# Sigmoid-gate products of two groups as 64-row pairs inside the up burst, with the attention stages two steps later

## The chip, the cores and the metric

The kernel runs on one core of a Trainium2 chip. The metric is the device time of one execution in microseconds (us), as the median of several runs. The engines are TensorE (PE in the profile; its weight loads are PEld), VectorE (DVE), ScalarE (ACT), GpSimd (POOL) and SyncE (SP, which issues the transfers here). Each engine takes its own instructions in the order in which the program gives them, and waits on semaphores for the others.

## The reference

The input x has the shape (4, 12608, 128). First comes an attention through 32 inducing vectors, then a channel mix in which every token also sees the one before it:

```python
def _attn_ref(x, inducing):
    def mab(q, kv):
        s = scale * (q @ kv.transpose(0, 2, 1)); s = s - s.max(-1, keepdims=True)
        a = np.exp(s); a /= a.sum(-1, keepdims=True) + 1e-09
        return a @ kv
    h = mab(I, x)              # 32 inducing vectors look at all tokens of a batch
    return mab(x, h)           # every token looks at the 32 results

def _moe_ref(x, mu_k, mu_r, w_k, w_v, w_r):
    x_prev = ...               # x moved by one token
    xk = mu_k * x + (1.0 - mu_k) * x_prev
    xr = mu_r * x + (1.0 - mu_r) * x_prev
    k = np.maximum(xk @ w_k, 0.0)          # d_ff = 1024
    v = k * k @ w_v
    r = 1.0 / (1.0 + np.exp(-(xr @ w_r)))  # the sigmoid gate
    return r * v
```

## The kernel before

**Groups, units, steps.** The tokens of a batch are cut into 25 groups of 512 tokens (the last one of a batch has 320). Since every token is a mix of only 32 results h, the products with w_k and w_r are folded into products of h with them: a token is represented by its 32 attention weights and by those of the token before it, 64 rows in all. These rows, as a rounded part (index 0) and the rest (index 1), lie in the tile R of the group, and twice: in partitions 0 to 63 and again in 64 to 127. The folded weights W (for k, as W[0] and W[1]) and Wg (for the gate) have 64 rows and lie twice likewise.

A group has 4 units of work, for 256 of the 1024 hidden columns each. The main loop has one step n for each unit, 400 in all (4 batches of 25 groups of 4). In the loop a step does, in this order in the program of each engine: `gate` of a finished group on DVE (L823); in even steps the *burst* of `up` products of this and the next unit on PE (L788); the `early` events of the step (registered with `soon`); `square` (L798 relu on DVE, L803 and L805 squares on ACT, or L800 on DVE in place of L803 in the steps of `high_vector`; then the difference kl on POOL, L808); in the second step of a group, `zgate`; `store` (L834); the `down` products of the unit of four steps ago on PE (L818); and the `events` of the step (registered with `at`).

`up` has 6 matmuls of 64 rows per unit: three terms (W[0] by R part 0, W[1] by part 0, W[0] by part 1), each once on rows 0 to 63 and once on rows 64 to 127, into the two banks of a `ps_a` tile. That makes 12 per burst of two units. `down` has 6 matmuls of 128 rows per unit, into the group's bank `ps_v`. `zgate` has 2 matmuls of 128 rows (L776) into the same `ps_v` bank, which the sigmoid (L778) empties into rT before the group's first `down` fills it again. The lower half of Wg holds the rest of the upper half there, so that 128 rows give two of the terms at once.

**PSUM.** It has 8 banks: two `ps_a` tiles of two banks, two `ps_v` banks in turn, `pb_a` and `pb_b`. A tile that is asked for under a name whose only bank is in use makes its first writer wait for the last reader of the tile before.

**The attention stages.** They run in the same loop, on a calendar. A batch b has segments of 12 steps (`SEG`); segment j begins at step s = 100b + 12j (4 + 12j for b = 0). I call n - s the place of step n in its segment. In segment j, `stage_a(b + 1, j)` works on block j (four groups) of the next batch, and `stage_b(b, j + 1)` makes the R tiles of block j + 1 of this one.

- Stage A with its offsets from s: four DVE transposes `btr` and their transfers to xt on SP (-1, 0, 1, 3); `scores` (9) on PE into `pb_a` (L367), its maximum on DVE; `expo` (15, early) on ACT, which reads `pb_a` (L403, L404); `etrans` (16) on DVE; `hmm` (17) on PE into a new `pb_a` (L436); `acc` (19) on DVE, which reads it. Offsets of 12 and more fall in the next segment. The last block has a tail (`t_tr` at 8 in `pb_a`, `t_scores`, `t_etrans` in `pb_b`).
- Stage B from s + 1: `scores` (0) on PE into `pb_b` (L617), then softmax on DVE in `pb_b` with its exponential (3, at the end of the step) on ACT (L634), `high` on ACT (7 after s), `low` on DVE (10 after s), then `spread`: transfers on SP that fill R of a new group, and two steps later `double`, which copies the upper 64 rows to the lower. R has 5 buffers, so `spread` of group f waits for the last reader of group f - 5.
- After the six segments of a batch `combine` makes h and the folded weights of the next one in `pb_b` and `pb_a`.

The 31 table loads at L778 in the profile are ACT's change from the set of functions with exp to the one with sigmoid.

Of the kernel before, what the change touches and what calls it, by code (L numbers as in the profile page):

```python
# [8 lines left out]
F32 = mybir.dt.float32  # L9
# [10 lines left out]
def kernel(  # L20
# [43 lines left out]
    banks = iter("ab" * 64)  # L64

    def pb_tile(bank=None):
# [142 lines left out]
    def stage_a_head(j):  # L209
# [34 lines left out]
        def scores():  # L244
            L.s1 = pv.tile([P, G], F32, name="ps_v")
# [75 lines left out]
    def stage_a(b, j, at, t):  # L321
# [139 lines left out]
        at(t + 10 + tail, common)  # L461
        at(t + 11 + tail, running)
        soon(t + 15, expo)
        at(t + 16, etrans)
        if tail:
            at(t + 16, t_etrans)
        at(t + 17, sums)
        at(t + 17, lambda: hmm(0))
        at(t + 17, lambda: hmm(1))
        at(t + 17, t_hmm)  # L470
        at(t + 19, acc)
        k = order_a.index((b, j))
# [8 lines left out]
    def combine(b, at=None, t=0):  # L481
# [45 lines left out]
        def hfin():  # L527
            ps = pb_tile("b")
            nc.tensor.matmul(out=ps[:, :M], lhsT=S.acc, rhs=L["sw"], start=True, stop=True)
            S.hT = sm.tile([P, M], F32, name="hT")  # L530
            nc.vector.tensor_copy(out=S.hT, in_=ps[:, :M])
            h4 = L["h4"] = sm.tile([P, Q, M], F32, name="h4", bufs=1)
            for n, mu in enumerate((muk, omuk, mur, omur)):
                nc.vector.tensor_scalar(out=h4[:, n, :], in0=ps[:, :M], scalar1=mu, scalar2=None, op0=ALU.mult)
            S.W = [wp.tile([P, F // 2], F32R, name=f"W{s}") for s in range(2)]
            S.Wg = wp.tile([P, C], F32R, name="Wg")

        def wpart(gate, tile):


            X = {}
            cw = C if gate else F // 2
            rows = slice(HP if gate else 0, P)

            def prod():
                X["ps"] = tile()[:, :cw]
                chunks = wk_sb.rearrange("p (c e d) -> p e c d", e=2, d=P)
                for n in range(Q):
                    o = X["ps"][M * n:M * (n + 1), :]
                    if not gate:  # L550
                        o = o.rearrange("m (c d) -> m c d", d=P)
                    nc.tensor.matmul(out=o, lhsT=L["h4"][:, 2 * gate + n % 2, :],
                                     rhs=wr_sb if gate else chunks[:, n // 2], start=True, stop=True)

            def high():
                nc.scalar.copy(out=(S.Wg if gate else S.W[0]), in_=X["ps"])

            def low():
                hi, lo = (S.Wg, S.Wg) if gate else S.W
                nc.vector.tensor_tensor(out=lo[rows], in0=X["ps"][rows], in1=hi.bitcast(F32)[rows],  # L560
                                        op=ALU.subtract)
            return prod, high, low

        if ahead:
            return maxes, weights, weights_sum, hfin, wpart
        at(t + 8, weights)
        at(t + 9, hfin)
        for gate in range(2):
            prod, high, low = wpart(gate, lambda: pb_tile("a"))
            at(t + 10 + 2 * gate, prod)  # L570
            at(t + 10 + 2 * gate, high)
            at(t + 11 + 2 * gate, low)

# [185 lines left out]
    NG = (NBLK - 1) * Q + 1  # L759
    UB = NG * NU  # L760

    class Group:
        def __init__(self, b, g):
# [4 lines left out]
            self.v = None  # L768

        def zgate(self):  # L770

            S, w = self.S, self.w
            R = S.R[self.g]
            ps = self.v = pv.tile([P, G], F32, name="ps_v")[:, :w]
            for s in range(2):
                nc.tensor.matmul(out=ps[:, :w], lhsT=S.Wg, rhs=R[:, s, :w], start=(s == 0), stop=(s == 1))  # L776
            self.rT = mp.tile([P, G], F32, name="rT")[:, :w]
            nc.scalar.activation(out=self.rT, in_=ps[:, :w], func=AF.Sigmoid)  # L778

        def up(self, u):  # L780
# [3 lines left out]
            ps = self.ps[u] = pa.tile([P, UC, G], F32, name="ps_a")  # L784
            for n, (a, k) in enumerate(((0, 0), (1, 0), (0, 1))):
                for r in range(2):
# [23 lines left out]
        def down(self, u):  # L810
            w = self.w
            if self.v is None:
                self.v = pv.tile([P, G], F32, name="ps_v")[:, :w]
            kh, kl = self.h.pop(u)
# [10 lines left out]
        def store(self):  # L825
# [10 lines left out]
            if g % span == span - 1 or g == NG - 1:  # L836
# [132 lines left out]
    def start():  # L969

        def bank():
            return pv.tile([P, G], F32, name="ps_v")

        wk = wpart(0, bank)
        wg = wpart(1, bank)
        (sc0, df0, ex0, nm0, turn0, hi0, lo0, idle), *rest = [stage_b_first(g) for g in range(Q)]
# [37 lines left out]
    end = len(units) - 1  # L1014
    late = []
    with tc.manual_schedule():
        head()
        start()
        for n in range(len(units) + LAG + 2):
            grp, u = units[n] if n < len(units) else (None, n % NU)  # L1020
            old, ou = units[n - LAG] if LAG <= n < len(units) + LAG else (None, 0)
            m = n - LAG - 1
            if 0 <= m < len(units) and units[m][1] == NU - 1:
                units[m][0].gate()
            if grp is None:
                run(late)
                late = []
            else:
                if n % 2 == 0:
                    for g, v in units[n:n + 2]:  # L1030
                        g.up(v)
                run(early.pop(n, []))
                whole = n in (end - 3, end - 1, end)
# [7 lines left out]
            if 1 <= m <= len(units) and units[m - 1][1] == NU - 1:  # L1041
                units[m - 1][0].store()
            if old is not None:
# [32 lines left out]
```

## Time and profile before

| | |
|---|---|
| median of 3 runs | 1096.88 us (1095.34 to 1097.85) |
| the profiled execution | 1095.42 us, span 1093.4 us |
| granted TensorE clock, mean | 0.999 |
| PE busy | 1068.4 us (98%), 6622 matmuls |
| DVE, ACT, POOL busy | 909.0, 961.2, 944.2 us (83, 88, 86%) |

The profile is of one execution; its own time is 1.46 us under the median. A busy PE is counted from matmuls that overlap in their records, so that the time from one start to the next is what a matmul costs when they follow each other.

### The profile page before, as it was taken

How to read it: one execution, taken by the hardware profiler on the slowest of the kernel's cores; microseconds unless marked ns; L12 is line 12 of the kernel's file. 1: busy time of each engine (PE TensorE's matmuls, PEld its weight loads, DVE VectorE, ACT ScalarE, POOL GpSimd, SP SyncE). 2: the span in 40 equal slices, each digit the busy share in tenths (PEclk: the TensorE clock that was granted, in tenths of full speed). 3: DMA queues.
4: the chain of work that ended last, by engine and by line, in shares of the span. 5: the costliest groups of instructions: out<-in, count | busy, mean ns of one | idle time of the engine just before them, and what ended most of it. 6: DMA issues, size and time to landing. Idle time of an engine off the chain costs nothing.

```text
span 1093.4 us, 19337 instructions
## 1 busy us (share of the span) xinstructions
PE 1068.4 (98%) x6622; PEld 735.1 (67%) x6622; DVE 909.0 (83%) x1296; ACT 961.2 (88%) x1101; POOL 944.2 (86%) x419
## 2 busy tenths in 40 slices
PE   7889999999999999999999999999999999999998
PEld 5456666666676666666676666666767666667776
DVE  4799899997788999997778899998786888887665
ACT  5498989898999889898999888999989989999996
POOL 2278988898889988989888989889889899999996
PEclk9999999999999999999999999999999999999999
DMA  9305676674157576665245746764415434453422
GB/s 280 118 8 116 157 158 163 142 157 100 27 113 168 122 163 134 145 156 126 41 75 121 171 109 150 176 149 102 86 28 108 83 59 93 85 101 70 89 40 35
DMA packets 267634, 123.61 MB, mean 113 GB/s; under 512 B 225648, under 2 KB 247056, under 8 KB 265232
## 3 DMA queue, kind: packets, MB, share of 16 engines
q1 hardware_dynamic: 267200, 122.35, 50.9%
q8 instruction: 53, 0.87, 0.4%
q14 instruction: 45, 0.37, 0.1%
q10 hardware_dynamic: 336, 0.02, 0.0%
HBM read 28.07 MB, written 25.82 MB: 49 GB/s over the span
## 4 chain that ended last, share of the span: by engine, by line
PE 84%; ACT 6%; DVE 3%; issue 2%; POOL 2%; SPq 1%; DMA 1%; ACTq 0%; DVEq 0%; POOLq 0%
PE ps_v L818 49%; PE ps_a L788 25%; PE ps_v L776 4%; ACT kh L803 2%; PE pb_b L617 2%; POOL kl L808 2%; PE pb_a L367 2%; PE pb_a L436 2%; ACT k_t L805 1%; DVE k_t L798 1%; DMA kl<-in_x_dram 1%; SPq L188 1%; ACT L778 1%; SPq L95 1%; ACT L634 0%
## 5 line engine op out<-in xcount | busy, mean ns | idle before, releaser
L808 POOL TENSOR_TENSOR kl<-k_t,kh 128x1024 fp32r<-128x1024 f32 (+1 forms) x397 | 932.6, 2386 | 105.8 <-ACT k_t L805 98.5
L798 DVE TENSOR_SCALAR k_t<-ps_a 128x1024 f32<-128x1024 f32 (+1 forms) x400 | 477.1, 1198 | 97.1 <-PE ps_a L788 74.7
L805 ACT ACTIVATE k_t<-k_t 128x1024 f32<-128x1024 f32 (+1 forms) x397 | 415.2, 1050 | 51.5 <-DVE kh L800 18.1
L803 ACT ACTIVATE kh<-k_t 128x1024 fp32r<-128x1024 f32 (+1 forms) x352 | 365.1, 1037 | 44.4 <-DVE k_t L798 41.7
L788 PE MATMUL ps_a<-R,W 64*128 64x512 f32 (+1 forms) x2400 | 331.1, 407 | 5.2 <-DVE k_t L798 4.5
L788 PEld LDWEIGHTS ps_a<-R,W 64*128 64x128 f32 x2400 | 208.7, 184 | 126.6 <-issue 49.5
L818 PE MATMUL ps_v<-kh,wvh 128*128 128x512 f32 (+1 forms) x800 | 270.3, 419 | 2.1 <-ACT rT L778 2.1
L818 PE MATMUL ps_v<-kh,wvl 128*128 128x512 f32 (+1 forms) x800 | 248.6, 392 | 0.0
L818 PE MATMUL ps_v<-kl,wvh 128*128 128x512 f32 (+1 forms) x800 | 248.5, 392 | 0.0
L818 PEld LDWEIGHTS ps_v<-kh,wvh 128*128 128x128 f32 x800 | 133.8, 188 | 93.0 <-issue 48.7
L818 PEld LDWEIGHTS ps_v<-kh,wvl 128*128 128x128 f32 x800 | 149.7, 188 | 34.9
L818 PEld LDWEIGHTS ps_v<-kl,wvh 128*128 128x128 f32 x800 | 149.5, 188 | 34.9
L823 DVE TENSOR_TENSOR oT<-ps_v,rT 128x512 f32<-128x512 f32 (+1 forms) x100 | 66.9, 669 | 20.4 <-PE ps_v L818 20.2
L834 DVE STREAM_TRANSPOSE ot<-oT 128x512 f32<-128x512 f32 x96 | 66.9, 697 | 0.0
L776 PE MATMUL ps_v<-R,Wg 128*128 128x512 f32 (+1 forms) x200 | 63.3, 398 | 0.0
L800 DVE SCALAR_TENSOR_TENSOR kh<-ps_a,k_t 128x1024 fp32r<-128x1024 f32 x48 | 58.8, 1225 | 1.7
L778 ACT ACTIVATE rT<-ps_v 128x512 f32<-128x512 f32 (+1 forms) x100 | 57.9, 579 | 0.3
L339 DVE STREAM_TRANSPOSE xs<-xb 128x512 f32<-128x512 f32 x72 | 49.9, 693 | 0.6 <-DMA xb<-in_x_dram 0.2
L776 PEld LDWEIGHTS ps_v<-R,Wg 128*128 128x128 f32 x200 | 36.5, 188 | 8.6 <-issue 0.8
L778 ACT ACT_TABLE_LOAD x31 | 39.8, 1283 | 0.6
L617 PE MATMUL pb_b<-xt,hT 128*32 128x512 f32 x184 | 24.4, 603 | 1.0 <-DVE R L749 1.0
L663 DVE TENSOR_TENSOR hl<-pb_b,hl 128x512 fp32r<-128x512 f32 x23 | 15.8, 688 | 7.0 <-ACT hl L660 6.7
(216 smaller groups left out, 527.0 us busy)
## 6 DMA issues: line engine op xcount, KB each, us to landing
out_dram<-ot SPq DMA_DIRECT2D x184, 128.0 KB, 2.7
R<-R SPq DMA_DIRECT2D x88, 256.0 KB, 3.0
xb<-in_x_dram SPq DMA_DIRECT2D x18, 1024.0 KB, 5.5
xt<-xs SPq DMA_DIRECT2D x288, 64.0 KB, 2.0
R<-hl SPq DMA_DIRECT2D x96, 128.0 KB, 2.3
R<-hl SPq DMA_DIRECT2D x96, 127.8 KB, 2.4
kh<-in_x_dram SPq DMA_DIRECT2D x4, 512.0 KB, 7.9
kl<-in_x_dram SPq DMA_DIRECT2D x4, 512.0 KB, 7.4
```

Source lines behind the costliest of these rows:

```text
L339: nc.vector.transpose(out=xs.rearrange("p (s q) -> p s q", q=M), in_=S.xb[j][:, :, M * c:M * (c + 1)])
L776: nc.tensor.matmul(out=ps[:, :w], lhsT=S.Wg, rhs=R[:, s, :w], start=(s == 0), stop=(s == 1))
L778: nc.scalar.activation(out=self.rT, in_=ps[:, :w], func=AF.Sigmoid)
L788: nc.tensor.matmul(out=ps[:, r, :w], lhsT=S.W[a][rows, u * P:(u + 1) * P], rhs=R[rows, k, :w], start=(n == 0), stop=(n == 2))
L798: nc.vector.tensor_scalar(out=k, in0=ps, scalar1=0.0, scalar2=None, op0=ALU.max)
L800: nc.vector.scalar_tensor_tensor(out=kh, in0=ps, scalar=0.0, in1=k, op0=ALU.max, op1=ALU.mult)
L803: nc.scalar.activation(out=kh, in_=k, func=AF.Square)
L805: nc.scalar.activation(out=k2, in_=k, func=AF.Square)
L808: return lambda: eng.tensor_tensor(out=kl, in0=k2, in1=kh.bitcast(F32), op=ALU.subtract)
L818: nc.tensor.matmul(out=self.v, lhsT=wt[:, fc, :], rhs=kk[:, c, :], start=(fc == 0 and n == 0), stop=(fc == FC - 1 and n == 2))
L823: nc.vector.tensor_tensor(out=self.oT, in0=self.v, in1=self.rT, op=ALU.mult)
L834: nc.vector.transpose(out=ot[:, o:o + w], in_=self.oT)
```

## The change

The gate products leave the 128-row form. For groups 2 to 99 they are made for two groups at once, in `zpair`: three terms, each one matmul for the first group on rows 0 to 63 and one for the second on rows 64 to 127, right behind the 12 `up` matmuls of a burst. That is in the steps n = 14, 22, 30 and so on up to 398 (n mod 8 = 6), the second group's third step. Groups 0 and 1 keep `zgate`, now with three 64-row matmuls. Wg becomes two full tiles, rounded part and rest.

The first group's product goes to `ps_v1`, the second's to `pb_a`, or to `pb_b` where the place of the step is 2 in the segments 1 to 6 of the batches 0 to 2 (and the last pair's first product to `pb_b`). The two sigmoids follow on ACT behind `square` of the same step. The two `ps_v` banks become two names with one bank each, by parity of the group. `gate` and `store` of the first group of a pair come two steps later.

Stage A moves by two steps from `scores` on (`scores` 11, `expo` 17 early, `etrans` 18, `hmm` 19, `acc` 21); its transposes move to 1, 2, 3 and 7, and the tail's `t_tr` to 5. Stage B starts at s + 3 with its exponential early in step s + 6; `combine` moves by two, and the first stage B of a batch starts two steps later and is packed closer. The steps of `high_vector` go from s + 4 and s + 8 to s + 6 and s + 10 (s + 7 for s + 10, where s + 6 has a pair).

```diff
-    pv = ctx.enter_context(tc.tile_pool(name="pv", bufs=2, space=bass.MemoryType.PSUM))
+    pv = ctx.enter_context(tc.tile_pool(name="pv", bufs=1, space=bass.MemoryType.PSUM))
...
+    def pv_tile(side=None):
+        return pv.tile([P, G], F32, name=f"ps_v{next(sides) if side is None else side % 2}")
...
-            at(t + ((-1, 0, 1, 3) if (b, j) != (1, 0) else (4, 5, 6, 7))[c], lambda c=c: btr(c))
+            at(t + ((1, 2, 3, 7) if b > 1 or j > 1 else (-1, 0, 1, 3) if j else (4, 5, 6, 7))[c], lambda c=c: btr(c))
         if tail:
-            at(t + 8, t_tr)
-            soon(t + 11, t_scores)
-        at(t + 9, scores)
+            at(t + 5, t_tr)
+            soon(t + 13, t_scores)
+        at(t + 11, scores)
...
-        soon(t + 15, expo)
-        at(t + 16, etrans)
+        soon(t + 17, expo)
+        at(t + 18, etrans)
...
-        at(t + 17, lambda: hmm(0))
-        at(t + 17, lambda: hmm(1))
+        at(t + 19, lambda: hmm(0))
+        at(t + 19, lambda: hmm(1))
...
-        at(t + 19, acc)
+        at(t + 21, acc)
...
-            S.Wg = wp.tile([P, C], F32R, name="Wg")
+            S.Wg = [wp.tile([P, C], F32R, name=f"Wg{s}") for s in range(2)]
...
+    TERMS = ((0, 0), (1, 0), (0, 1))
...
+        def zpart(self, ps, a, k, rows, n):
+            nc.tensor.matmul(out=ps, lhsT=self.S.Wg[a][rows, :], rhs=self.S.R[self.g][rows, k, :self.w],
+                             start=(n == 0), stop=(n == len(TERMS) - 1))
...
         def zgate(self):
-            for s in range(2):
-                nc.tensor.matmul(out=ps[:, :w], lhsT=S.Wg, rhs=R[:, s, :w], start=(s == 0), stop=(s == 1))
+            for n, (a, k) in enumerate(TERMS):
+                self.zpart(ps, a, k, slice(0, HP), n)
...
+    def zpair(n, two):
+        last = two[1].b == B - 1 and two[1].g == NG - 1
+        r = n - (0 if n >= UB else 4)
+        spot = r % UB
+        side = "b" if r < (B - 1) * UB and SEG <= spot < 7 * SEG and spot % SEG == 2 else "a"
+        ps = [pb_tile("b") if last else pv_tile(two[1].b * NG + two[1].g), pb_tile(side)]
+        ps = [t[:, :grp.w] for grp, t in zip(two, ps)]
+        for m, (a, k) in enumerate(TERMS):
+            for h in range(2):
+                two[h].zpart(ps[h], a, k, slice(HP * h, HP * (h + 1)), m)
+        return lambda: run([lambda grp=grp, t=t: grp.sigmoid(t) for grp, t in zip(two, ps)])
...
-            high_vector |= {s + 4, s + 8}
+            high_vector |= {s + 6, s + (7 if (s + 6) % (2 * NU) == NU + 2 else 10)}
...
-                stage_b(b, j + 1, at, s + (1 if j != (b == 0) else -3 if b else -1))
+                stage_b(b, j + 1, at, s + (3 if j != (b == 0) else -3 if b else -1), early=soon, offsets=(0, 1, 1, 2, 3, 5, 5, 6, 7, 7, 9))
...
-            stage_b(b + 1, 0, at, s + 10)
+            stage_b(b + 1, 0, at, s + 12, offsets=(0, 1, 1, 2, 3, 4, 4, 5, 5, 6, 7))
...
+    for k in range(0, len(units), NU):
+        n = k + NU + LAG + (2 if k % (2 * NU) == 0 and NU < k < len(units) - 2 * NU else 0)
+        gates.setdefault(n, []).append(units[k][0])
+        stores.setdefault(n + 1, []).append(units[k][0])
...
+                if n % (2 * NU) == NU + 2 and n > 2 * NU:
+                    sig = zpair(n, (units[n - NU - 2][0], units[n - 2][0]))
                 run(early.pop(n, []))
                 whole = n in (end - 3, end - 1, end)
                 low = grp.square(u, n in high_vector, whole)
...
-                if n >= 2 * NU and u == 1:
-                    grp.zgate()
...
+                if sig:
+                    sig()
```

More of the change, by code (lines that the diff above doesn't have):

```diff
@@ L244, in scores @@
         def scores():
-            L.s1 = pv.tile([P, G], F32, name="ps_v")
+            L.s1 = pv_tile()
             for i in range(Q):
@@ L555, in high @@
             def high():
-                nc.scalar.copy(out=(S.Wg if gate else S.W[0]), in_=X["ps"])
+                nc.scalar.copy(out=(S.Wg if gate else S.W)[0], in_=X["ps"])
             def low():
-                hi, lo = (S.Wg, S.Wg) if gate else S.W
-                nc.vector.tensor_tensor(out=lo[rows], in0=X["ps"][rows], in1=hi.bitcast(F32)[rows],
-                                        op=ALU.subtract)
+                hi, lo = S.Wg if gate else S.W
+                nc.vector.tensor_tensor(out=lo, in0=X["ps"], in1=hi.bitcast(F32), op=ALU.subtract)
             return prod, high, low
@@ L565, in combine @@
             return maxes, weights, weights_sum, hfin, wpart
[L566 to L567 removed]
+        at(t + 10, weights)
+        at(t + 11, hfin)
         for gate in range(2):
             prod, high, low = wpart(gate, lambda: pb_tile("a"))
[L570 to L572 removed]
+            at(t + 12 + 2 * gate, prod)
+            at(t + 12 + 2 * gate, high)
+            at(t + 13 + 2 * gate, low)
     def new_r(S, g, src=None, copies=1):
@@ L768, in __init__, with bank, sigmoid @@
             self.v = None
-        def zgate(self):
-            S, w = self.S, self.w
-            R = S.R[self.g]
-            ps = self.v = pv.tile([P, G], F32, name="ps_v")[:, :w]
-            for s in range(2):
-                nc.tensor.matmul(out=ps[:, :w], lhsT=S.Wg, rhs=R[:, s, :w], start=(s == 0), stop=(s == 1))
-            self.rT = mp.tile([P, G], F32, name="rT")[:, :w]
-            nc.scalar.activation(out=self.rT, in_=ps[:, :w], func=AF.Sigmoid)
+        def bank(self):
+            if self.v is None:
+                self.v = pv_tile(self.b * NG + self.g)[:, :self.w]
+            return self.v
+        def zpart(self, ps, a, k, rows, n):
+            nc.tensor.matmul(out=ps, lhsT=self.S.Wg[a][rows, :], rhs=self.S.R[self.g][rows, k, :self.w],
+                             start=(n == 0), stop=(n == len(TERMS) - 1))
+        def sigmoid(self, ps):
+            self.rT = mp.tile([P, G], F32, name="rT")[:, :self.w]
+            nc.scalar.activation(out=self.rT, in_=ps, func=AF.Sigmoid)
+        def zgate(self):
+            ps = self.bank()
+            for n, (a, k) in enumerate(TERMS):
+                self.zpart(ps, a, k, slice(0, HP), n)
+            self.sigmoid(ps)
         def up(self, u):
@@ L784, in up @@
             ps = self.ps[u] = pa.tile([P, UC, G], F32, name="ps_a")
-            for n, (a, k) in enumerate(((0, 0), (1, 0), (0, 1))):
+            for n, (a, k) in enumerate(TERMS):
                 for r in range(2):
@@ L810, in down @@
         def down(self, u):
-            w = self.w
-            if self.v is None:
-                self.v = pv.tile([P, G], F32, name="ps_v")[:, :w]
+            self.bank()
             kh, kl = self.h.pop(u)
@@ L969, in start @@
     def start():
[L971 to L975, printed above, removed]
+        wk = wpart(0, pv_tile)
+        wg = wpart(1, pv_tile)
         (sc0, df0, ex0, nm0, turn0, hi0, lo0, idle), *rest = [stage_b_first(g) for g in range(Q)]
@@ L1021 @@
             old, ou = units[n - LAG] if LAG <= n < len(units) + LAG else (None, 0)
-            m = n - LAG - 1
-            if 0 <= m < len(units) and units[m][1] == NU - 1:
-                units[m][0].gate()
+            for grp_ in gates.pop(n, []):
+                grp_.gate()
             if grp is None:
@@ L1038 @@
                     low()
-                if n >= 2 * NU and u == 1:
-                    grp.zgate()
-            if 1 <= m <= len(units) and units[m - 1][1] == NU - 1:
-                units[m - 1][0].store()
+                if sig:
+                    sig()
+            for grp_ in stores.pop(n, []):
+                grp_.store()
             if old is not None:
```

14 lines of the change are left out of this document (8 added, 6 removed).

## The prediction

> **What bounds the kernel now.** I read the page first, then the chain that ended last, then stretches of the main loop, then the timeline of one period by engine.
>
> ```profile
> span 1093.4 us, 19337 instructions
> PE 1068.4 (98%) x6622; PEld 735.1 (67%) x6622; DVE 909.0 (83%) x1296; ACT 961.2 (88%) x1101; POOL 944.2 (86%) x419
> PE 84%; ACT 6%; DVE 3%; issue 2%; POOL 2%; SPq 1%; DMA 1%; ACTq 0%; DVEq 0%; POOLq 0%
> ```
> ```profile
> core 0: us, PE busy (x) PEld busy (x) DVE busy (x) ACT busy (x) POOL busy (x), PEclk, DMA share, GB/s
> 397.10:429.06 31.96, 31.96 (x202) 21.64 (x198) 29.93 (x44) 28.77 (x32) 28.57 (x13) 1.00 0.68 151
> 848.50:1080.00 231.50, 230.44 (x1216) 161.17 (x1216) 179.72 (x204) 213.14 (x226) 222.70 (x94) 1.00 0.38 74
> ```
>
> PE carries 84% of the chain. A segment of 12 steps of the first three batches takes 31.96 us and PE is busy for all of it; ACT is busy for 28.77, DVE for 29.93. In the last batch, without stage A, POOL has 222.70 of 231.50, so it is nearly a second bound there. In the loop, then, each slot that PE saves is worth its full time, and each wait put into PE's queue costs its full time.
>
> **What a product costs on PE.** This is PE from step 126 on, a burst (L788) and the `down` products behind it; step 129 holds an old gate product (L776) and `hmm` (L436).
>
> ```profile
> 386.44 1.67 PE L788 MATMUL ps_a<-R,W 64*128 64x512 f32 x12
> 388.04 0.74 PE L818 MATMUL ps_v<-kh,wvh 128*128 128x512 f32 x2
> 388.62 0.63 PE L818 MATMUL ps_v<-kh,wvl 128*128 128x512 f32 x2
> 389.08 0.63 PE L818 MATMUL ps_v<-kl,wvh 128*128 128x512 f32 x2
> ...
> 391.04 1.66 PE L788 MATMUL ps_a<-R,W 64*128 64x512 f32 x12
> 392.63 0.73 PE L818 MATMUL ps_v<-kh,wvh 128*128 128x512 f32 x2
> ...
> 394.13 0.63 PE L776 MATMUL ps_v<-R,Wg 128*128 128x512 f32 x2
> 394.60 0.63 PE L818 MATMUL ps_v<-kh,wvh 128*128 128x512 f32 x2
> ...
> 396.09 1.08 PE L436 MATMUL pb_a<-xb,e 128*32 128x128 f32 x32
> 397.10 1.67 PE L788 MATMUL ps_a<-R,W 64*128 64x512 f32 x12
> ```
>
> Two 128-row products take 0.46 to 0.47 us from start to start, 0.233 each: one slot. Twelve 64-row products take 1.60 us with the change of form behind them, six slots and 0.2: two halves on different rows share a slot. With U for the start of a burst (386.44), the first `down` starts at U + 1.6, and the second step's `down` products end at U + 4.6.
>
> **What is saved.** Before: 100 groups of two slots, 200. After: 49 pairs of three slots, 147, and 2 groups of three 64-row products with nobody on the other rows, 6. That is 47 slots, 10.9 us. The pair has the burst's form and adds no change of form. In the last batch (12 pairs, 2.8 us) POOL leaves room for about half, so I take off 1.4; the narrow tail groups and the last pair, whose two sigmoids stand before the last square, take some 0.3. Saved: 9.2 us.
>
> ```profile
> L776 PE MATMUL ps_v<-R,Wg 128*128 128x512 f32 (+1 forms) x200 | 63.3, 398 | 0.0
> L778 ACT ACTIVATE rT<-ps_v 128x512 f32<-128x512 f32 (+1 forms) x100 | 57.9, 579 | 0.3
> L778 ACT ACT_TABLE_LOAD x31 | 39.8, 1283 | 0.6
> ```
>
> The L776 row's 63.3 us is no better price: its records overlap. Sigmoids stay 100, and about one table load to exp and one back per segment stay too, so ACT's sum stays.
>
> **What is added: short leases on banks.** The pair's second product sits in `pb_a` or `pb_b`, and there PE's next user comes at the end of the next step. When is the sigmoid done by then? ACT in the same two steps (DVE's relu and ACT's squares of step 126, then `expo` of stage A, early in step 127):
>
> ```profile
> 387.52 1.22 DVE L798 TENSOR_SCALAR k_t<-ps_a 128x1024 f32<-128x1024 f32 x1 [1.11 <-PE ps_a L788]
> ...
> 391.14 0.70 DVE L339 STREAM_TRANSPOSE xs<-xb 128x512 f32<-128x512 f32 x1
> ```
> ```profile
> 388.78 1.06 ACT L803 ACTIVATE kh<-k_t 128x1024 fp32r<-128x1024 f32 x1 [0.48 <-DVE k_t L798]
> 389.94 1.06 ACT L805 ACTIVATE k_t<-k_t 128x1024 f32<-128x1024 f32 x1
> 391.01 1.28 ACT L403 ACT_TABLE_LOAD   x1
> 392.31 0.29 ACT L403 ACTIVATE alpha<-mkr,nb 128x1 f32<-128x1 f32 x1
> 392.51 0.67 ACT L404 ACTIVATE e1t<-pb_a,nb 128x512 f32<-128x512 f32 x1
> 393.08 0.19 ACT L404 ACTIVATION_READ_ACCUMULATOR e1t<-pb_a,nb 128x1 f32 x1
> 393.17 1.05 ACT L803 ACTIVATE kh<-k_t 128x1024 fp32r<-128x1024 f32 x1
> 394.31 2.24 ACT L805 ACTIVATE k_t<-k_t 128x1024 f32<-128x1024 f32 x2
> 396.46 0.61 ACT L634 ACTIVATE s<-s 128x512 f32<-128x512 f32 x1
> ```
>
> Relu waited only for PE and ends at U + 2.3, the second square at U + 4.56. This is a floor: what stands behind `square` of the burst's first step on ACT cannot start earlier, with DVE's square of a `high_vector` step neither. Two sigmoids behind it (0.58 each, the next one starting 0.1 before the end, as alpha and e1t do) end at U + 4.6 + 0.5 + 0.6 = U + 5.7, with a table load (1.28) at U + 7.0. PE is through the pair (0.7), the change of form and both steps' `down` products at U + 5.3. So PE waits 0.4 us, or 1.7 with a load. The old gate had until three steps on. The places, going through the calendar:
>
> - Place 10, then `scores` of stage A at place 11 in `pb_a`. The exponentials of places 5 and 6 have brought the exp table, so a load: n = 38, 62, 134, 158, 222, 246, 270, 7 x 1.7 = 11.9. At n = 14 and 110 no exponential has come between: 0.4 each.
> - Place 2, then `scores` of stage B at place 3 in `pb_b`, no load: n = 30, 54, 126, 150, 214, 238, 262. With the two before, 9 x 0.4 = 3.6.
> - Place 6 has two waits. The pair needs `pb_a` free of `expo`, now early in place 5; e1t ends at 392.51 + 0.67 = U + 6.74, the pair is due at U + 4.6 + 1.5 = U + 6.1: 0.65. Then `hmm` at place 7 needs the sigmoid. ACT from e1t on: squares of place 5 to U + 8.9, stage B's exponential 0.55, the square of place 6 1.06, load 1.28, sigmoids 1.1: U + 12.9. PE: 6.74 + 0.7 + 0.1 + 3.0 = U + 10.5. Wait 2.4. Together 3.05, at n = 46, 118, 142, 230, 254, 278: 18.3. At n = 22 no load comes before the exponential, and stage B's is elsewhere: only `hmm` waits, 1.6.
> - `t_tr`, now at t + 5, takes `pb_a` in the step whose early event is `expo`: 6.74 - 4.6, about 2.2, at n = 69, 165, 265. In the pairs of 70 and 166 the late PE finds the bank free and waits 0.85 for `hmm`. Sum 3 x 2.2 + 2 x 0.85 = 8.3.
> - n = 286: the second product of `combine` in `pb_a` at the end of the same step, PE there at U + 3.8, sigmoids at U + 5.7: 1.9.
>
> Such waits exist already, where a group's first `down` finds the sigmoid late. Those rows prove that PE stands still for it, and the third shows that POOL gains nothing by it, since it waits for ACT.
>
> ```profile
> PEld ps_v L818 <- ACT rT L778: 6.9, 13, 1.1
> PE ps_v L818 <- ACT rT L778: 2.1, 3, 0.7
> POOL kl L808 <- ACT k_t L805: 98.5, 76, 10.7
> ```
>
> **SP's queue.** R of an even group is now read until n = 4g + 6, while `spread` of group g + 5 is in SP's order from 4g + 3. SP stands there about three steps, with transfers behind it.
>
> ```profile
> 391.94 2.44 SPq L342 DMA_DIRECT2D xt<-xs  x4
> 394.42 1.23 SPq L591 DMA_DIRECT2D R<-R  x2
> 395.70 0.67 SPq L584 DMA_DIRECT2D R<-hl  x1
> 396.41 1.79 SPq L597 DMA_DIRECT2D R<-hl  x2
> ```
> ```profile
> xt<-xs SPq DMA_DIRECT2D x288, 64.0 KB, 2.0
> ```
>
> R itself is due 14 steps after the pair, outputs have a spare tile: nothing. But where `btr` 3 at place 7 shares the step with such a `spread` (n = 59, 155, 243, 267), the last xt transfer is issued at U + 2.3 + 7 x 0.61 less one, and lands 2.0 later, U + 8, against `scores` at U + 7.0: 1.0 each, 4.0.
>
> The other moves (`gate` and `store` two steps later, `high_vector`, `combine`) I cost at nothing: DVE and ACT have 2 to 3 us spare per segment, and PE's waits give them more. If that cover is gone, relu comes late, and every floor above moves with it.
>
> **The sum.** Waits 11.9 + 3.6 + 18.3 + 1.6 + 8.3 + 1.9 + 4.0 = 49.6. The profiled execution: 1095.4 - 9.2 + 49.6 = 1135.8, say 1136, 3.6% over it; the median before is 1.5 higher than that execution. Bounds of the waits: half of them, if PE comes later to the banks than reckoned, 25, gives 1111; DVE late by 0.7 (a transpose before relu) at each of the 27 places adds 19 and gives 1155. That is the likeliest case's own range.
>
> **The rivals.** (1) The waits do not appear, because the sigmoids are done when PE comes. For it: ACT is 10% idle and PE waits for sigmoids only 2.1 us before. Against: the floor of U + 4.56 is latency, not load. The sum would be 1095.4 - 9.2 = 1086, faster. It decides at 9.2 us: with waits of under a fifth of mine, the change gains. (2) Waits between, 5 to 15 us, so that they about cancel the saving: 1091 to 1101. It needs ACT to have its square before U + 3, which the relu's row excludes. (3) The pair's halves share a slot only in part, since they read two R tiles: at 1.3 slots a pair of halves the 147 slots become 191, 10 us more, 1146. (4) They do not share at all: 294 slots, 34 us more, 1170. Against both: the burst above, whose halves read different rows and write different banks as well, takes six slots for twelve.
>
> The Trainium skill, "TensorE: Matmul & The Clock Gate", Part 3, tells of four row tiles that ran 3.07 times as fast as one, not 4, which as an estimate is the 1.3 slots of rival 3. The 1.60 us of twelve halves say one slot, and I go by them.
>
> **Chances.** Forecast, waits of 25 to 70 us: 0.72. Rival 1: 0.14. Rival 2: 0.07, of which faster 0.03, the same 0.03, slower 0.01. Rival 3: 0.04. Rival 4: 0.03. The three runs before lie within 0.2%, so less than that is no change: faster 0.17, same 0.03, slower 0.80. The range leaves out rivals 1 and 4: 1091 to 1155.
>
> **What would show it.** Right: idle time of PE before `scores`, `hmm` and the pair, put down to rT and e1t of ACT; PE busy at about 1058 in a longer span; 294 gate products in threes of 0.23 us per pair; waits of SP for PE before `spread`. Wrong: PE's share at 98% still, with a span near 1084 (the banks were free in time), or pairs of more than 0.8 us (rivals 3 and 4). The step I am least sure of is `hmm` at place 7, where five ACT instructions add up.

## The result, and the profile after

| | before | after |
|---|---|---|
| median | 1096.61 us (1095.34 to 1097.85, 4 runs) | 1183.13 us (1180.83 to 1185.98, 4 runs) |
| the profiled execution | 1095.42 us, span 1093.4 | 1180.83 us, span 1179.0 |
| granted TensorE clock, mean | 0.999 | 0.983 |

The changed kernel takes 1.079 times as long (1.0759 to 1.0822): 86.5 us more, where 40 were forecast. The sign is as predicted, and the time lies outside the range.

The page of the changed kernel (span, busy time and share of each engine, shares of the chain that ended last):

```profile
span 1179.0 us, 19549 instructions
PE 1089.9 (92%) x6722; PEld 739.2 (63%) x6722; DVE 904.3 (77%) x1296; ACT 966.5 (82%) x1101; POOL 945.1 (80%) x419
PE 44%; DVE 21%; ACT 19%; issue 8%; SPq 4%; DMA 3%; DVEq 0%; ACTq 0%
```

PE falls from 98% of the span to 92%, and from 84% of the chain to 44%. DVE had 3% of it and now has 21%. The work of DVE, ACT and POOL is the same within 6 us each: nothing became heavier, things became later.

Two stretches of the changed kernel, a middle segment (steps 130 to 141) and the last batch without its end (304 to 395); the columns after the stretch are its length and the busy time of each engine:

```profile
core 0: us, PE busy (x) PEld busy (x) DVE busy (x) ACT busy (x) POOL busy (x), PEclk, DMA share, GB/s
425.85:461.72 35.87, 33.29 (x200) 22.35 (x199) 30.38 (x44) 28.39 (x32) 28.54 (x12) 0.95 0.59 133
933.71:1161.20 227.49, 224.21 (x1211) 155.22 (x1210) 173.66 (x199) 208.72 (x221) 219.47 (x94) 1.00 0.38 74
```

The segment took 31.96 us before and takes 35.87. The 92 steps of the last batch took 227.56 (from the start of one burst to that of another) and take 227.49. So the whole loss lies in the three batches with stage A: there the bursts lose 85.2 us up to step 304, and from there to the end of the kernel 0.4.

What PE waits for in the changed kernel (us in total, times, longest; rT is a pair's sigmoid, e1t the exponential of stage A; L372 is `scores` of stage A, L620 of stage B, L441 `hmm`, L352 `t_tr`, L781 the pair, L831 `down`, L556 the product of `combine`):

```profile
PE pb_a L441 <- ACT rT L786: 15.7, 9, 2.9
PE pb_a L372 <- ACT rT L786: 15.4, 8, 2.6
PE ps_v L831 <- ACT rT L786: 8.2, 8, 1.9
PE pb_b L620 <- ACT rT L786: 8.2, 7, 1.3
PE pb_a L352 <- ACT e1t L409: 7.3, 3, 2.6
PE pb_a L372 <- DMA R<-R: 2.5, 1, 2.5
PE pb_a L781 <- ACT e1t L409: 2.3, 6, 0.4
PE pb_a L556 <- ACT rT L786: 2.2, 1, 2.2
```

These are the forecast's places, and one row that it did not have (`down`, 2.1 us before). The row with a transfer is no place of its own: it is the pair of n = 222, at place 10 like six others. `scores` does not read that R, and it starts when the sigmoid has emptied its bank:

```profile
693.43 0.59 ACT L786 ACTIVATE rT<-pb_a 128x512 f32<-128x512 f32 x1
...
694.08 2.33 PE L372 MATMUL pb_a<-xt,indT 128*32 128x512 f32 x8 [2.55 <-DMA R<-R]
```

So 17.9 us of `scores` of stage A are waits for rT. The waits are real and where they were expected; their sum is not the whole loss.

One of the seven pairs of place 10, n = 134, with its burst at U = 436.02:

```profile
436.02 1.73 PE L803 MATMUL ps_a<-R,W 64*128 64x512 f32 x12
436.65 0.70 DVE L847 STREAM_TRANSPOSE ot<-oT 128x512 f32<-128x512 f32 x1
...
437.27 0.31 DVE L456 SCALAR_TENSOR_TENSOR acc<-acc,alpha,pb_a 128x128 f32<-128x128 f32 x1
437.50 0.68 DVE L648 TENSOR_TENSOR s<-s,pb_b 128x512 f32<-128x512 f32 x1
437.59 0.39 PE L781 MATMUL ps_v<-R,Wg 64*128 64x512 f32 x1
...
438.10 1.22 DVE L813 TENSOR_SCALAR k_t<-ps_a 128x1024 f32<-128x1024 f32 x1
438.21 0.39 PE L781 MATMUL pb_a<-R,Wg 64*128 64x512 f32 x1
...
438.52 0.74 PE L831 MATMUL ps_v<-kh,wvh 128*128 128x512 f32 x2
...
439.35 1.22 DVE L815 SCALAR_TENSOR_TENSOR kh<-ps_a,k_t 128x1024 fp32r<-128x1024 f32 x1
...
440.67 1.06 ACT L820 ACTIVATE k_t<-k_t 128x1024 f32<-128x1024 f32 x1 [1.62 <-DVE kh L815]
...
441.74 1.28 ACT L786 ACT_TABLE_LOAD   x1
...
443.04 0.60 ACT L786 ACTIVATE rT<-ps_v 128x512 f32<-128x512 f32 x1
443.53 0.59 ACT L786 ACTIVATE rT<-pb_a 128x512 f32<-128x512 f32 x1
...
444.18 1.45 PE L372 MATMUL pb_a<-xt,indT 128*32 128x512 f32 x8 [2.58 <-ACT rT L786]
...
445.56 2.93 PE L803 MATMUL ps_a<-R,W 64*128 64x512 f32 x12
```

Two things here are not in the forecast. The relu (L813) starts at U + 2.08, not at U + 1.08: `store` (L847), `acc` (L456) and a product of stage B (L648) stand ahead of it on DVE. And the burst behind the wait takes 2.93 us for the work of 1.67.

### The profile page after: what moved, and what is told of

The parts are those of the page before. It is cut to its first block, busy times and chain, and to the rows that moved or that the text cites. A ratio compares the mean times of both kernels' runs of the same rounds, so it can differ in the third digit from the quotient of the medians.

```text
span 1179.0 us, 19549 instructions
## 1 busy us (share of the span) xinstructions
PE 1089.9 (92%) x6722; PEld 739.2 (63%) x6722; DVE 904.3 (77%) x1296; ACT 966.5 (82%) x1101; POOL 945.1 (80%) x419
## 4 chain that ended last, share of the span: by engine, by line
PE 44%; DVE 21%; ACT 19%; issue 8%; SPq 4%; DMA 3%; DVEq 0%; ACTq 0%
PE ps_v L831 23%; PE ps_a L803 14%; DVE k_t L813 11%; ACT kh L818 5%; ACT k_t L820 5%; ACT rT L786 3%; ACT L786 2%; PE pb_a L372 2%; DVE ot L847 1%; PE pb_b L620 1%; PE pb_a L441 1%; DVE kh L815 1%; SPq L854 1%; DVE oT L836 1%; DMA out_dram<-ot 1%
## 5 line engine op out<-in xcount | busy, mean ns | idle before, releaser
L813 DVE TENSOR_SCALAR k_t<-ps_a 128x1024 f32<-128x1024 f32 (+1 forms) x400 | 475.1, 1197 | 142.9 <-PE ps_a L803 134.4
L803 PE MATMUL ps_a<-R,W 64*128 64x512 f32 (+1 forms) x2400 | 343.2, 416 | 7.9 <-DVE k_t L813 6.5
L803 PEld LDWEIGHTS ps_a<-R,W 64*128 64x128 f32 x2400 | 212.9, 189 | 137.9 <-issue 50.0
L831 PE MATMUL ps_v<-kh,wvh 128*128 128x512 f32 (+1 forms) x800 | 273.3, 423 | 8.4 <-ACT rT L786 8.2
L831 PE MATMUL ps_v<-kh,wvl 128*128 128x512 f32 (+1 forms) x800 | 249.1, 393 | 0.0
L831 PE MATMUL ps_v<-kl,wvh 128*128 128x512 f32 (+1 forms) x800 | 248.6, 392 | 0.0
L831 PEld LDWEIGHTS ps_v<-kh,wvh 128*128 128x128 f32 x800 | 134.2, 189 | 102.2 <-issue 62.1
L831 PEld LDWEIGHTS ps_v<-kh,wvl 128*128 128x128 f32 x800 | 150.7, 189 | 35.1
L831 PEld LDWEIGHTS ps_v<-kl,wvh 128*128 128x128 f32 x800 | 149.7, 188 | 34.9
L847 DVE STREAM_TRANSPOSE ot<-oT 128x512 f32<-128x512 f32 x96 | 66.8, 696 | 0.0
L375 DVE TENSOR_REDUCE mx<-pb_a 128x1 f32<-128x512 f32 x18 | 12.5, 692 | 44.6 <-PE pb_a L372 44.6
L781 PE MATMUL ps_v<-R,Wg 64*128 64x512 f32 (+1 forms) x150 | 45.4, 404 | 0.0
L372 PE MATMUL pb_a<-xt,indT 128*32 128x512 f32 x144 | 26.7, 670 | 18.0 <-ACT rT L786 15.4
L781 PE MATMUL pb_a<-R,Wg 64*128 64x512 f32 (+1 forms) x120 | 36.3, 410 | 2.3 <-ACT e1t L409 2.3
L441 PE MATMUL pb_a<-xb,e 128*32 128x128 f32 x576 | 20.2, 282 | 15.7 <-ACT rT L786 15.7
```

What stands on the lines that cost most here:

```text
L372: nc.tensor.matmul(out=ps[M * i:M * (i + 1), :], lhsT=indT, rhs=S.xt[j, i], start=True, stop=True)
L781: nc.tensor.matmul(out=ps, lhsT=self.S.Wg[a][rows, :], rhs=self.S.R[self.g][rows, k, :self.w], start=(n == 0), stop=(n == len(TERMS) - 1))
L803: nc.tensor.matmul(out=ps[:, r, :w], lhsT=S.W[a][rows, u * P:(u + 1) * P], rhs=R[rows, k, :w], start=(n == 0), stop=(n == 2))
L813: nc.vector.tensor_scalar(out=k, in0=ps, scalar1=0.0, scalar2=None, op0=ALU.max)
L831: nc.tensor.matmul(out=self.v, lhsT=wt[:, fc, :], rhs=kk[:, c, :], start=(fc == 0 and n == 0), stop=(fc == FC - 1 and n == 2))
L847: nc.vector.transpose(out=ot[:, o:o + w], in_=self.oT)
```

## The experiments

My theory after the first reading: the loss is waits for the banks, raised by a late relu; a half clock that follows them; and a cost of the new calendar by itself. The main rival is that the pairs themselves, or the calendar alone, make up the whole. The kernel before stood at 1095.9 to 1096.1 us beside these runs.

### The calendar alone

The kernel before with the new offsets of the stages, `high_vector` and `combine`, but the old gate products in their old place:

```diff
-            at(t + 8, t_tr)
+            at(t + 5, t_tr)
...
-        at(t + 9, scores)
+        at(t + 11, scores)
...
-            high_vector |= {s + 4, s + 8}
+            high_vector |= {s + 6, s + (7 if (s + 6) % (2 * NU) == NU + 2 else 10)}
```

> The kernel before with the new calendar alone (stage A, stage B, combine, high_vector as after), its gate products and sigmoids as they were. Theory (the pairs' short leases of pb_a and pb_b cost the time, by PE's waits and by the half clock that follows them): the waits of PE for rT before scores and hmm are gone, the three waits of t_tr for e1t (2.5 us each) and some 8 us between the batches stay: 1105 to 1115 us, at most three stretches of half clock. Rival (the moved stages themselves make DVE and ACT late): most of the loss stays, over 1150 us.

Measured: 1118.92 us, ratio 1.0207 (1.0192 to 1.0223), 22.8 us more, above the theory's range. Its table loads and waits (line, times | busy; then the waits as above):

```profile
L778 ACT ACT_TABLE_LOAD x45 | 57.7, 1283 | 0.8
L634 ACT ACT_TABLE_LOAD x27 | 34.6, 1283 | 0.5
```
```profile
PE pb_a L347 <- ACT e1t L404: 6.8, 3, 2.4
PE ps_a L788 <- DVE kh L800: 3.6, 5, 1.1
PEld ps_a L788 <- DVE k_t L798: 22.2, 48, 1.8
```

6.8 us are `t_tr`, a term of the forecast. The rest was costed at nothing. Part of it belongs to this mixture alone: with the old gates in the new calendar ACT changes its table 28 times more often (45 and 27 loads, where 31 and 13 stand before and after). So I take what is left as an upper bound of the calendar's own cost.

Two parts of it were then undone, each alone. First the steps of `high_vector`:

```diff
-            high_vector |= {s + 6, s + (7 if (s + 6) % (2 * NU) == NU + 2 else 10)}
+            high_vector |= {s + 4, s + 8}
```

> This is the kernel before with the new calendar of stages A and B and the old gates (1118.9 us), but with the two squares on VectorE back in places 4 and 8 of a segment, where the kernel before has them. Theory: the moved squares carry part of the calendar's 22.8 us. In places 6 and 7 of every second segment both fall into one burst's pair of steps; each reads the burst's bank, so the next burst waits for them (3.6 us in 5 waits for kh of VectorE, 9.0 us of waits of PE's weight loads for the same, both 0 before), and the relu behind comes late. I expect 1109 to 1115 us. Rival: the squares do not matter, what costs is where the matrix products of stage A stand, so 1117 to 1120 us; or the squares in places 4 and 8 now collide with other work of VectorE, and it is slower than 1120 us.

Measured: 1116.34 us, 1.0185 (1.0171 to 1.0199). A miss: 2.6 us instead of 4 to 10. The waits for kh went, and waits for the relu took their place, in the weight loads:

```profile
PEld ps_a L788 <- DVE k_t L798: 36.7, 75, 1.1
```

75 waits instead of 48: in the new calendar the old steps are as crowded on DVE. Then the tail's transpose:

```diff
-            at(t + 5, t_tr)
+            at(t + 10, t_tr)
```

> The same calendar with the old gates, and the tail's transpose t_tr at step 10 of its segment in place of 5, as far ahead of scores as in the kernel before. Theory: t_tr at step 5 asks for the bank pb_a in the step in which expo has only begun to read it; its three waits for e1t (6.8 us), and the half clock of 3.4 us behind one of them (1.3 us or so lost), go away: 1118.9 - 8 = 1111 us (1109 to 1113). Rival: the transpose then waits for acc or delays scores by as much, 1116 to 1120 us.

Measured: 1108.94 us, 1.0116 (1.0102 to 1.013): 10.0 us less. `t_tr`, next to a bank that is being read, cost its three waits and what came behind them. The calendar's other moves cost 13 us in this mixture, 5.0 of them between the batches (steps 80 to 103, 176 to 205, 282 to 303).

### What the waits are made of

The sigmoids ahead of the squares of their step:

```diff
                 run(early.pop(n, []))
+                if sig:
+                    sig()
                 whole = n in (end - 3, end - 1, end)
...
-                if sig:
-                    sig()
```

> After, with the two sigmoids of a pair put on ACT ahead of the squares of their step in place of behind them. Theory: the sigmoids end near U + 4.7, ahead of PE's next use of the bank at U + 5.3, so the 55 us of waits fall to the ten of t_tr and of the pair itself, the half-clock stretches fall from 11 to at most 3, and the squares come 1.1 to 2.4 us later, which the 3 to 8 us that kl is early by take: 1110 to 1125 us. Rival (the loss is ACT's and DVE's load, the order within a step does not matter): over 1160 us.

Measured: 1136.24 us, 1.0361 (1.0346 to 1.0377): 46.9 us less by ACT's order alone, though not the 58 to 73 of the theory. Its waits:

```profile
PE pb_a L441 <- ACT rT L786: 6.7, 7, 1.1
...
PE pb_a L372 <- ACT k_t L820: 2.0, 2, 1.0
...
PE pb_a L372 <- ACT kh L818: 1.2, 1, 1.2
...
PE pb_a L372 <- DMA xt<-xs: 1.0, 1, 1.0
```

`scores` of stage A waits 4.2 us instead of 17.9, and what it waits for last is a square or a transfer; stage B's `scores` and the `down` products no longer wait for rT. So the squares ahead of the sigmoids were the larger part of the waits.

The changed kernel with an exponential in place of the sigmoid, so that the loop needs no table loads (it leaves out the gate's function):

```diff
-            nc.scalar.activation(out=self.rT, in_=ps, func=AF.Sigmoid)
+            nc.scalar.activation(out=self.rT, in_=ps, func=AF.Exp)
```

> The changed kernel with Exp in place of Sigmoid in the pairs, so that ScalarE loads no table in the loop (the gate's function is not computed). Theory: 13 of the waits of scores and hmm hold a table load of 1.28 us each between the squares and the sigmoids, 16.6 us in all; shorter by that, the pauses of TensorE stay under 2 us and the half clock windows (some 14 us) go as well: 1183.1 - 16.6 - 14 = 1152 us (1145 to 1160). Rival: the waits are set by the late relu on VectorE and the loads lie in time that ScalarE waits anyway: 1170 to 1183 us.

Measured: 1128.82 us, 1.0298 (1.0284 to 1.0312), 54.3 us less, more than expected.

```profile
PE pb_b L620 <- ACT rT L786: 8.1, 7, 1.3
PE pb_a L372 <- ACT rT L786: 7.6, 8, 1.2
PE pb_a L441 <- ACT rT L786: 5.5, 9, 1.0
```

`scores` and `hmm` wait 19.3 us less (17.9 + 15.7 against 7.6 + 1.2 for a transfer + 5.5), somewhat more than the 16.6 of the 13 loads that the theory counted. Stage B's `scores`, whose pairs meet no load, wait as before (8.1 against 8.2). The 7.6 that stay before stage A's `scores` should have been 3.6 by the forecast's floor, 0.4 in each of nine places; the relu starts at U + 2.06 at most pairs of place 10 in this kernel too. The rest of the gain is mainly the waits of `down` (8.2, gone), shorter ones of `t_tr` (3.5 instead of 7.3) and of the pair (gone), and the half clock, 2 windows in the loop instead of 11.

The half clock by itself: the changed kernel with 9, 7 or 8 products on PE whose result nobody reads, ahead of those `scores`, `hmm` and `t_tr` that wait:

```diff
         def scores():
+            if (t + 11) % 8 == 7:
+                busy(9)
             ps = pb_tile("a")
```

> After, with products that nobody reads (9, 7 and 8 of 0.233 us, into a ps_a buffer) put on PE ahead of stage A's scores, of hmm and of t_tr where these wait. They lie inside the waits of 2.0 to 2.7 us. Theory (a good part of the loss, some 17 us, is PE's clock at half for 3.4 us after such a wait): the waits for the banks end at the same time as before, the half-clock stretches go, and more work on PE makes it faster: 1164 to 1172 us. Rival (what is slow behind a wait is the refilling of the other engines, the clock is no cause): 1181 to 1190 us.

Measured: 1173.04 us, 1.0698 (1.0682 to 1.0714): with 168 products more it is 10.1 us faster (7.0 between the two profiled spans). That is 1.0 above the theory's range and far from the rival's. The burst behind the wait of n = 134 in it, with the added products at L943:

```profile
443.46 2.23 PE L943 MATMUL ps_a<-wvh 128*128 128x512 f32 x9
...
446.21 1.38 PE L375 MATMUL pb_a<-xt,indT 128*32 128x512 f32 x8 [0.53 <-ACT rT L791]
...
447.52 1.67 PE L808 MATMUL ps_a<-R,W 64*128 64x512 f32 x12
```

The wait for rT ends as late as before, and the burst is back at 1.67 us. Burst by burst against the changed kernel, 9 of the 11 places with a half clock gain 1.3 to 1.7 us, 13.7 in all; the other two gain nothing, since PE waits there anyway. Against that, the added products cost 1.3 us each at n = 14 and 110, where the wait was short, and the clock fell at two other places.

`scores` and `hmm` one step later, away from the pair:

```diff
-        at(t + 11, scores)
+        at(t + 12, scores)
...
-        at(t + 19, lambda: hmm(0))
+        at(t + 20, lambda: hmm(0))
```

> After, with stage A's scores one step later (12) and hmm one step later (20), all else the same. Theory: one more step of down products, 1.4 us, and at scores also the next burst, 1.6 us, stand between the pair and the next use of its bank: the waits before scores (2.65 each) fall under 0.4, those before hmm (2.1) under 0.5, eight of 11 half-clock stretches go; the waits of stage B's scores, of t_tr and of the pair stay: 1130 to 1145 us. Rival (DVE's and ACT's load decides): the waits reappear at the new places, over 1165 us.

Measured: 1168.79 us, 1.0669 (1.0651 to 1.0687). A miss: the rival's range. The waits of both for rT are gone, as the theory said, and another has come. The first line is from the list of waits, the others lie around the burst of n = 138, which starts at 447.58:

```profile
PE ps_a L803 <- DVE k_t L813: 17.2, 23, 2.1
```
```profile
446.19 0.69 DVE L375 TENSOR_REDUCE mx<-pb_a 128x1 f32<-128x512 f32 x1 [2.33 <-PE pb_a L372]
...
447.46 0.69 DVE L666 TENSOR_TENSOR hl<-pb_b,hl 128x512 fp32r<-128x512 f32 x1
...
448.07 1.22 DVE L813 TENSOR_SCALAR k_t<-ps_a 128x1024 f32<-128x1024 f32 x1
...
449.43 0.95 PE L803 MATMUL ps_a<-R,W 64*128 64x512 f32 x6 [0.89 <-DVE k_t L813]
```

The maximum of the scores (L375) comes a step later with them, and it and what follows it stand ahead of the relu on DVE; the second half of the burst waits for that relu's bank. A stage that is moved to spare PE a wait brings its DVE work along.

### Undoing the causes together

The sigmoids first, `t_tr` at 10, and `expo` one step earlier:

```diff
-            at(t + 5, t_tr)
+            at(t + 10, t_tr)
...
-        soon(t + 17, expo)
+        soon(t + 16, expo)
```

> The changed kernel with three steps taken together: the sigmoids ahead of the squares of their step (alone 1136.2 us), t_tr at step 10 of its segment in place of 5 (in the calendar without pairs it gave 10.0 us), and expo of stage A one step earlier, so that ScalarE has its exponentials and their table load behind it when the pair of place 6 comes. Theory: the gains add, 1136.2 - 10 - 6.7 (waits of hmm for rT) - 2.2 (waits of the pair for e1t) = 1117 us (1112 to 1122); what is left over the kernel before is then the calendar's order on VectorE, 13 us in the run with t_tr moved alone, and waits of under 1 us, and the 11 us that the pairs save on TensorE stay invisible. Rival: with expo earlier its wait moves to the running maximum on VectorE, and the relu comes late for it: 1124 to 1135 us.

Measured: 1123.58 us, 1.0251 (1.0233 to 1.0269), just beyond the theory's range. `hmm` still waits (11.9 us in 9 waits for rT), and something else had come to light at n = 158:

```profile
488.02 2.44 SPq L347 DMA_DIRECT2D xt<-xs  x4
...
490.05 3.02 PE L372 MATMUL pb_a<-xt,indT 128*32 128x512 f32 x8 [0.96 <-ACT k_t L820]
```

`scores` takes 3.02 us instead of 1.06, since its rows are still landing: the wait for SP's queue that the forecast had put at 1.0 us in four places. So the last transposition went two steps forward:

```diff
-            at(t + ((1, 2, 3, 7) if b > 1 or j > 1 else (-1, 0, 1, 3) if j else (4, 5, 6, 7))[c], lambda c=c: btr(c))
+            at(t + ((1, 2, 3, 5) if b > 1 or j > 1 else (-1, 0, 1, 3) if j else (4, 5, 6, 7))[c], lambda c=c: btr(c))
```

> The combined kernel (1123.6 us) with the fourth transposed quarter of a block's rows (btr 3) at step 5 of its segment in place of 7, so at the same distance to scores as in the kernel before. Theory: with the sigmoids out of the way it is the queue of SP that holds scores up; from first to last start its eight products take 0.47 us in the kernel before and 1.8 to 2.4 us at five places of the combined kernel (n = 62, 134, 158, 246, 270), where the rows' transfers land while scores runs, 8.6 us in all; this goes, and with it some idle time in front of scores: 1114 us (1111 to 1117). Rival: the transposition at place 5 stands ahead of a relu on VectorE or its transfers behind a spread there, and the time stays at 1120 to 1126 us.

Measured: 1115.37 us, 1.0176 (1.0157 to 1.0194): 8.2 us less, as expected. At the five places `scores` is back at 0.47 us from its first to its last start. In the changed kernel most of this lay within the wait of `scores` for rT: at these five places it takes 0.8 to 1.8 us from its first to its last start there, and 1.8 to 2.4 in the combined run. Last, stage B's exponential at the end of its step:

```diff
-                stage_b(b, j + 1, at, s + (3 if j != (b == 0) else -3 if b else -1), early=soon, offsets=(0, 1, 1, 2, 3, 5, 5, 6, 7, 7, 9))
+                stage_b(b, j + 1, at, s + (3 if j != (b == 0) else -3 if b else -1), offsets=(0, 1, 1, 2, 3, 5, 5, 6, 7, 7, 9))
```

> The same, and stage B's exponential of place 6 at the end of its step in place of the front, so behind the pair's sigmoids. Theory: hmm waits for the sigmoids 11.9 us in 9 waits in the combined kernel since that exponential (0.6 us) and the table load behind it (1.28 us) stand ahead of them; behind them, most of it goes: 10 us under the run with the rows early, 1104 us (1101 to 1109). Rival: the load is needed between the exponential of place 4 and the sigmoids in any case, and a further pair of loads comes behind, so it is the same or slower, 1112 to 1120 us.

Measured: 1121.75 us, 1.0233 (1.0215 to 1.0252), slower by 6.4: the rival, and just above its range. An exponential between two lots of sigmoids costs loads, 14 more than the 31 and 13 of the kernel before:

```profile
L786 ACT ACT_TABLE_LOAD x38 | 48.8, 1283 | 0.7
L637 ACT ACT_TABLE_LOAD x20 | 25.7, 1283 | 0.4
```

The Trainium skill, "ScalarE: Activation LUTs", section "Table sets: the hidden batching unit", asks to batch calls by table set; this run and that of the calendar alone agree, by the loads counted above.

### Is there a faster version?

Pairs in the last batch alone, where nobody else wants `pb_a`, with the calendar of the kernel before and the sigmoids first:

```diff
...
-                if n % (2 * NU) == NU + 2 and n > 2 * NU:
+                if n % (2 * NU) == NU + 2 and n > (B - 1) * UB + NU + 2:
                     sig = zpair(n, (units[n - NU - 2][0], units[n - 2][0]))
...
```

> The calendar of the kernel before for all stages, and pairs only in the last batch, where stage A has no work and so nobody else wants pb_a; their two sigmoids stand ahead of the squares of their step; the three earlier batches keep the old gate products. Theory: a pair saves one slot of 0.23 us where its second bank is free and nobody waits for it; 12 pairs give 2.8 us: 1093.3 us (1092.6 to 1094.6), faster than both kernels. Rival: POOL and ScalarE are nearly as busy as TensorE there, so the slots saved turn into waits for kl and rT: 1095.5 to 1097 us; or the sigmoids ahead of the squares delay the kl of every pair and it is over 1097 us.

Measured: 1096.69 us, 1.0006 (0.9997 to 1.0015): nothing, as the rival had it. Up to step 360 several bursts of each segment last 0.2 to 0.4 us longer and take the slot back, while PE's weight loads wait 22.7 us for the relu instead of 17.2; from 362 to 396 the pairs show their price undisturbed: the burst with a pair takes 5.29 us instead of 4.59, the two that lost a gate 4.59 instead of 5.05, 0.23 us less for a pair. With the new places of stage B and `high_vector` in that batch alone:

```diff
...
+            if b == B - 1 and j:
+                stage_b(b, j + 1, at, s + 3, early=soon, offsets=(0, 1, 1, 2, 3, 5, 5, 6, 7, 7, 9))
...
```

> Pairs in the last batch only, as in the run at 1096.7 us, and in that batch alone the new places of stage B and of VectorE's squares; the three earlier batches are those of the kernel before. Theory: in the last batch of the run with the sigmoids first the pairs gained 2.1 us from step 304 on with these places, against 0.1 us lost with the old ones, where relu came late by 0.2 to 0.4 us in every second burst; so 1096.7 - 2.2 = 1094.5 us (1093.8 to 1095.3), some 0.1% faster than before. Rival: POOL, busy for 222.7 of 231.5 us there, takes the slots back in any order: 1096 to 1097 us.

Measured: a median of 1095.11 us, 0.9992 (0.9982 to 1.0001). Its profile gains 2.0 us from step 304 on and loses 0.6 in step 300, whose group 75 has a gate of three products; a gain of 0.1% is likely, but the interval holds 1. With pairs in all batches the best was 1115.37 us.

## Why the prediction was right and wrong

**The saving.** Right in its price: 0.23 us for a pair where nothing disturbs it. In the last batch, where the forecast kept half of 2.8 us, nothing is left: its 92 steps take as long as before, and `down` waits 3.0 us for rT there instead of 0.7. Rivals 3 and 4 (the halves share a slot in part or not at all) are refuted by the 0.70 us of six halves, and rival 1 (no waits) by the list of waits.

**The waits.** Right in place, and near in their sum by the rows, 53.6 us against 49.6, but that nearness is partly luck: one term is 10.6 short, and 6.6 in the others did not come as waits. The terms, predicted and measured: `scores` of both stages 15.5 and 26.1; `hmm` 16.0 and 15.1; the pair for e1t 3.9 and 2.3; `t_tr` with the pairs behind it 8.3 and 7.9; `combine` 1.9 and 2.2; SP 4.0, and no wait of its own. What SP was to cost lies inside `scores`, whose eight products take 0.8 to 1.8 us from the first to the last start at the four places named, instead of 0.47. The row of `hmm`, the step that I was least sure of, came out, and by the five ACT instructions that were added up. The mis-sized term is `scores`. Its step was "Relu waited only for PE and ends at U + 2.3", read from one step of the kernel before, 126. In the changed kernel the relu starts at U + 2.07 (within 0.01) in five of the seven pairs of place 10 and at U + 2.25 in five of the seven of place 2, instead of U + 1.08 in the same steps before. The waits follow: counted from start to start, 2.65 us at place 10 where 1.7 was forecast, 1.41 at place 2 where 0.4 was. Where the relu still starts at U + 1.08, the forecast holds: the pair of n = 270, with a load, waits 1.87, those of n = 14 and 110, without one, 0.44. No run put the relu alone back in its place; the link rests on these rows.

**What was costed at nothing.** This is the step that failed. The moves of `store`, `high_vector` and `combine` were said to be covered by DVE's spare 2 to 3 us of a segment, and what the moved stages A and B do on DVE was not asked. A sum of spare time covers nothing if the moved instruction stands right in front of a relu in its queue. It shows twice: in the 10.6 us that `scores` waits beyond the forecast, and inside the bursts, whose second half waits for a late relu (once for DVE's square) to free its bank, 6.3 us more than before outside the half clock. In the run of the calendar with `t_tr` late, such waits inside the bursts, for the relu or for DVE's square, are 9.9 of the 13.9 us that its profiled span is longer. The prediction named it ("If that cover is gone, relu comes late, and every floor above moves with it"), but its upper bound of 1155 priced 0.7 us at each place and nothing else.

**What was not in the sum.** Two more things. PE's `down` products wait 6.1 us more for rT, in places that the list did not have. And the half clock costs 13.7 us, by the run with the added products.

**The whole.** The waits can also be counted from one PE product's start to the next one's, against the usual time between the same two products in the kernel before; idle rows miss a part, since the ends of matmuls are modelled. Counted so, the 85.6 us between the two spans are made up as follows:

| longer by | us |
|---|---|
| slots saved | -10.9 |
| before `scores` of stage A, of stage B | 18.6, 8.2 |
| before `hmm` | 16.3 |
| before `t_tr`, and before the product of `combine` | 7.7, 2.3 |
| in the pairs, most of it for e1t | 6.6 |
| before `down` | 7.7 |
| products that touch a window of half clock | 17.4 |
| inside the bursts, at full clock | 6.3 |
| inside `scores`, at full clock, while rows land | 2.8 |
| before another product of `combine`, which waits for DVE | 2.3 |
| the rest | 0.3 |

Of the 17.4 the added products took back 13.7. The places of the forecast, SP's among them, come to 62.5 us in this count against its 49.6; the half clock, `down` and the bursts, 31.4 us, are what its sum did not have.

**What would show it.** PE idle before `scores`, `hmm` and the pair, with rT and e1t as releasers: seen. PE busy at about 1058: wrong, 1089.9. Half-clock bursts last longer, and a `scores` whose rows are landing counts as busy all the while (L372 is busy for 26.7 us, before for 19.8), so waiting hides in busy time.

## What to carry to other kernels

A product that borrows a bank for a short lease is priced by the latency of the engine that empties the bank: go through that engine's queue at that very step, and through the queue of the engine that feeds it, step by step and not by their spare time in a segment. Put the instruction that frees the bank ahead of work that nobody waits for yet: here the order of two sigmoids and two squares was worth 47 of 87 us. When PE is the bound, a pause of 2 us can cost another 1.5 us behind it, and when a wait is taken away, look what it covered: here a transfer in one run, and in another a maximum on DVE that moved along.

## What the runs showed of the hardware

The half clock came without PE ever being idle for long: the longest single wait in the list is 2.9 us. The trace grants the clock in windows of 3.41 us on a fixed grid. Four of them in the changed kernel (third column: PE busy; the third from the right: granted clock):

```profile
394.14:397.55 3.41, 1.62 (x7) 0.96 (x6) 2.90 (x3) 3.38 (x5) 3.41 (x2) 1.00 0.57 114
397.55:400.96 3.41, 3.19 (x47) 2.35 (x48) 1.10 (x1) 1.12 (x2) 3.33 (x2) 1.00 0.34 81
441.93:445.34 3.41, 1.17 (x8) 0.47 (x8) 0.38 (x1) 3.40 (x5) 2.50 (x2) 1.00 0.63 255
445.34:448.75 3.41, 3.41 (x15) 2.17 (x14) 2.09 (x3) 1.45 (x3) 1.97 (x1) 0.50 0.02 5
```

After a window with 1.62 us of PE busy the clock stays at 1.00, after one with 1.17 it is 0.50 for a window. In the main loops of the kernel before, the changed one and the twelve experiments, every window at full clock with PE busy for under 0.45 of it was followed by half clock and none with over 0.53; between these it went either way. Behind a window that is itself at half clock this does not hold: in three of the experiments a second one followed although PE was busy for 0.62, 0.93 and all of the first. So a pause that the grid cuts into two windows can go free, and the added products fit this, since they filled a window. The share is read from the traces; the added products are the only run that was made to test it.

The Trainium skill, "TensorE: Matmul & The Clock Gate", section "What's actually happening", tells of a free-running window of 3413 ns and half rate after an idle window. The trace agrees on the length and the factor. The same page, "HAM oscillation — how this bites in real kernels", gives the rule of no PE idle gaps over some 3.4 us; by that rule nothing would have been lost here, and the measurement decides: waits of 2 to 2.9 us lost 13.7 us.
